# A down projection with seven block products in one period more, and the accumulators of both halves added up on GpSimd

## The chip, the cores and the metric

The kernel runs on one core of a Trainium2 chip. The metric is the device time of one execution in microseconds (us); three runs of the kernel before gave 1813.7, 1811.5 and 1813.31 us, median 1813.31. One further execution was profiled. In all that follows PE is TensorE (PEld its weight loads), DVE is VectorE, ACT is ScalarE, POOL is GpSimd, and SP is SyncE, which here only issues transfers.

## The reference

A block with a memory-augmented attention and, behind it, a feed-forward part; the change lies in the latter. With S = 2048 rows, D = 576 and F = 4608, all in float32:

```
h = _layernorm(x) * (1 + cb) + sb
g = silu(h @ w_gate)            # 2048 x 4608
u = h @ w_up
x = x + gb * ((g * u) @ w_down) # down projection, 2048 x 576
```

## The kernel before

The feed-forward part fills the time from about 640 us to the end. The 2048 rows are worked off in two halves of 1024, `t` = 0 and 1, and in each half the 4608 columns in 18 periods, `p` = 0 to 17 (`NPR` = 18), of 256 columns. A period has 14 steps, `k` = 0 to 13. In each step `step(z, m)` makes one of the seven products of a Strassen-Winograd scheme for gate (`z` = 0) or up (`z` = 1): seven matmuls of 128x512 into the PSUM banks A, B or C. `fin` makes from these the activations `sg`, and `prep_w` splits the weights for a step five steps ahead into a high part `wh` (ACT) and a low part `wl` (DVE, `wl <- O, wh`).

The down projection of a period is made one period later, between the steps. It too has two forms.

- `down`: seven block products. It has 14 chunks c, two for each of the products m in the order `POS` = 1, 4, 2, 5, 6, 7, 3. A chunk is six matmuls of 128x288 into a PSUM tile `pd` and one addition of `pd` to half of the accumulator `acc[m]`. In half 0 the odd chunks go another way: ACT loads the accumulator into PSUM beforehand (`preload`), the matmuls add to it, and ACT copies it back. The operands of the products are sums of blocks: `sum_a` (DVE) for the activations, `sum_d` (POOL, half 0 only) for the weights, which are then stored to DRAM for half 1.
- `plain`: the four blocks without the scheme. It has 8 chunks of twelve matmuls of 128x288, each followed by an addition on DVE into one of the four results `acc[2]`, `acc[3]`, `acc[4]` and `x11`.

Chunks alternate between two PSUM tiles, one buffer each (`dn0`, `dn1`), so chunk c+2 has to wait for the addition behind chunk c. Operands are split like the weights: `ah` and `dh` on ACT, `al <- sg, ah` and `dl <- dr, dh` on DVE. The tables CH, CH0, CHE and CHB say how many chunks follow each step.

Periods 0 to 15 use `down`, periods 16 and 17 use `plain`. Since `plain` adds to the four results, the seven accumulators have to be added up into these before: eight additions of 128x1152, `comb(t, j)` for j = 0 to 7, all on DVE, at steps 1 to 8 of period 17. They are acc2 += acc1, x11 += acc5, acc6 += acc1, acc5 += acc6, acc3 += acc5, acc7 += acc6, acc4 += acc7, x11 += acc7. The `plain` chunks of period 17 of half 0 are made in period 0 of half 1 ("across the border"); those of half 1 end the kernel, each followed by a store.

Everything is emitted in the order of this loop (the schedule is manual), so each engine works off its instructions in just that order. POOL has no instruction after period 17 of half 0.

Of the kernel before, what the change touches and what calls it, by code (L numbers as in the profile page):

```python
# [11 lines left out]
ALU = mybir.AluOpType  # L12
# [22 lines left out]
PF = 5  # L35
NSG = 7
CH = (1, 1, 1, 1, 2, 1, 0, 1, 1, 1, 1, 2, 1, 0)
CH0 = (0, 0, 0, 1, 1, 1, 1, 1, 1, 1, 1, 0, 0, 0)
CHE = (0, 0, 0, 0, 0, 1, 1, 1, 1, 1, 1, 1, 1, 0)
CHB = (0, 0, 1, 1, 1, 1, 1, 1, 1, 1, 0, 0, 0, 0)  # L40
# [32 lines left out]
RB = 9  # L73
RL = (-10, -1, 0, 4, 4, 9, 10, 10, 12, 10, 11, 12, 15, 16)
SUMS = ((4, 3, 2, ALU.add), (5, 4, 0, ALU.subtract), (3, 0, 3, ALU.subtract), (6, 1, 5, ALU.subtract))
S1B, S2B, XB, WB = 3, 3, 2, 1


# [5 lines left out]
def block(ctx: ExitStack, tc: tile.TileContext, x, wqk, wv, wo, beta, wgu, wgr, wd, c, crow, w_mod, w_mod0, w_mod1, w_modc, xt, out):  # L84
    nc = tc.nc
# [713 lines left out]
    op = pool(p2r, "op", side="right")  # L799
# [239 lines left out]
    NPR = NF // 2  # L1039
# [7 lines left out]
    def at(g, f):  # L1047
        sched.setdefault(g, []).append(f)
# [110 lines left out]
    def stage_r():  # L1159
        big = flat(yh12.rearrange("p a b c -> p (a b) c"))  # L1160
        ts = [big[:, 896 * i:896 * i + 896].rearrange("p (a b) -> p a b", b=P) for i in range(3)]
        for b in range(RB):
            o, h, g, w = ts[b % 2], ts[2].bitcast(F32R), 22 * b, b % (NF // 4)
            at(max(0, g + RL[0]), lambda w=w, o=o: nc.sync.dma_start(o[:, 0:4], wgr[w]))
            for j, (d, x_, y_, op) in enumerate(SUMS):
                at(max(0, g + RL[1 + j]), lambda o=o, d=d, x_=x_, y_=y_, op=op: nc.gpsimd.tensor_tensor(o[:, d], o[:, x_], o[:, y_], op=op))
# [135 lines left out]
    def sum_o(p, z, j, eng=nc.gpsimd):  # L1302
        o = O[p, z]
        d, a, b, op = SUMS[j]
        if eng is nc.vector:
# [15 lines left out]
    def load_d(t, p):  # L1321
# [4 lines left out]
        else:  # L1326
            nc.sync.dma_start(r[:, :NS[p]], wdD[p][:, :NS[p]])

# [99 lines left out]
        nc.vector.tensor_tensor(PA[d], PA[a], PA[b], op=op)  # L1428

    PA, acc, x11 = {}, {}, {}  # L1430
    NS = [7] * (NPR - 2) + [4] * 2

    def new_acc(accp, ms):
        for m in ms:
# [72 lines left out]
    def comb(t, j):  # L1507
        d, b = ((2, 1), (0, 5), (6, 1), (5, 6), (3, 5), (7, 6), (4, 7), (0, 7))[j]
        d = acc[d] if d else x11[t]
        nc.vector.tensor_tensor(d, d, acc[b], op=ALU.add)  # L1510

    def is_plain(t, p):
        return p >= NPR - 2

    with tc.manual_schedule():
        SB.append(S1B)
# [69 lines left out]
        for i in range(4):  # L1586
            for h in range(2):
                for c in range(WC):
# [5 lines left out]
                    if n in SS:  # L1594
                        j = SS.index(n)
# [33 lines left out]
        for t in range(2):  # L1629
            for p in range(NPR):  # L1630
                end = p == NPR - 1
                last = t == 1 and end
                dl = 2 if t == 0 and p == 0 else 0
                nx = (p + 1) % NPR
                tn = t if nx else t + 1
                if t == 0 and p == 1:
                    p7.close()
                    accq = pool(p4, "acq")
                    new_acc(accq, (1, 6, 7))
                    x2p = pool(p6, "x2p")  # L1640
                    g2 = prep2(x2p)
                if t == 0 and p == NPR - 1:
                    now[0] = PTK[0]
                    run(g2)
                    p6.close()
                if end:
                    load_x11(t)
                chunk = 0
                for k in range(14):
                    z, m = ZM[k]  # L1650
                    todo, later[:] = later[:], []
                    while nw < len(seq) and nw <= n + PF + (t == 0 and k == 7):
                        prep_w(*seq[nw])
                        nw += 1
                    n += 1
                    for f in todo:
                        f()
                    while outs:
                        outs.pop(0)()
                    if prev is not None and not is_plain(*prev):  # L1660
                        for c in range(chunk, chunk + CH[k] + CH[(k + 1) % 14]):
                            if not PRE:
                                preload(*prev, c)
                    while acts:
                        acts.pop(0)()
                    if dl and k in HP:
                        y_here(6 + HP.index(k))
                    if k != 1 or prev is not None:
                        step(z, m)
                    if k == 1 and prev is not None:  # L1670
                        PA[0, 1] = AC[0, 1]
                    if t == 0 and p == NPR - 1 and k in (7, 9, 10, 11, 12, 13) or t == 1 and p == 0 and k == 1:
                        load_y(1, ACT_OP[m])
                    swap = t == 1 and p == 0
                    if not last and k == (6 if swap else 7 - PF):
                        load_o(tn, nx, 0)
                        if dl:
                            for i in range(2):
                                nc.sync.dma_start(xD[3][:, 2 * i:2 * i + 2, :], x3[i])
                    elif not last and k == (14 - PF if tn else 8):  # L1680
                        load_o(tn, nx, 1)
                    if k == 2 + swap and (t or p):
                        load_r(p, 1)
                    elif not last and k == 9:
                        load_r(nx, 0)
                    if t == 0:
                        if k == 1 and p:
                            load_d(0, p)
                        elif not dl and k == 3:
                            mul_d(p, 0)  # L1690
                            mul_d(p, 1)
                        if not dl and k in (4, 5) and p < NPR - 2:
                            sum_d(p, 2 * k - 8)
                            sum_d(p, 2 * k - 7)
                        if tn == 0 and 5 <= k < 9:
                            sum_o(nx, 0, k - 5)
                        elif tn == 0 and k in (10, 11):
                            sum_o(nx, 1, 2 * k - 20)
                            sum_o(nx, 1, 2 * k - 19)
                        if k == 0 and p == 0:  # L1700
                            store_o(p, 0)
                            store_o(p, 1)
                        elif k == 11 and tn == 0:
                            store_o(nx, 0)
                        elif k == 13 and tn == 0:
                            store_o(nx, 1)
                        if k == (5 if end else 12 + dl // 2):
                            nc.scalar.dma_start(wdD[p][:, :NS[p]], RW[p][:, :NS[p]])
                    if t and k == 2 + 2 * swap:
                        load_d(1, p)  # L1710
                    if prev is not None and is_plain(*prev):
                        if k in (0, 2):
                            ij = (1, 0) if k == 0 else (0, 1)
                            prep_a(prev[1] % 2, ij, PA[ij])
                        if (CHE if t == 0 else CHB if p == 0 else CH0)[k]:
                            f = plain(*prev, chunk)
                            if f:
                                late[k + 3] = f
                            chunk += 1
                        due(k)  # L1720
                    elif prev is not None:
                        for j in range(4):
                            if k == KS[j]:
                                sum_a(j)
                        if k == 0:
                            prep_a(prev[1] % 2, 2, PA[1, 0])
                        for j, kk in KA:
                            if k == kk:
                                prep_a(prev[1] % 2, j, PA[ASRC[j]])
                        for _ in range(CH[k]):  # L1730
                            down(*prev, chunk)
                            chunk += 1
                    if end and 1 <= k < 9:
                        comb(t, k - 1)
                    if p == 0 and (t, k) in RS:
                        load_res(t, RS[t, k])
                    if is_plain(t, p):
                        if k in DK[t == 0 and end]:
                            j = DK[t == 0 and end].index(k)
                            prep_d(p, (j // 2, j % 2), j)  # L1740
                    elif k >= 7:
                        prep_d(p, POS[k - 7], WSLOT[POS[k - 7]])
                    for ij, kk, j in (((0, 0), 11, 1), ((1, 1), 13, 4)):
                        if k == kk:
                            prep_a(p % 2, ij if is_plain(t, p) else j, AC[ij])
                    now[0] = k
                    if t == 0 and k in G2 and p > 1:
                        next(g2, None)
                for k in sorted(late):
                    due(k)  # L1750
                PA.clear()
                PA.update(AC)
                prev = (t, p)
# [86 lines left out]
```

## Time and profile before

| | us |
|---|---|
| median of three runs | 1813.31 |
| profiled execution, its time | 1815.41 |
| its span | 1813.4 |
| PE busy in the span | 1786.3 (99%) |
| DVE busy | 1485.3 (82%) |
| ACT busy | 1086.7 (60%) |
| POOL busy | 672.6 (37%) |
| end of half 0's period 17, start of half 1 | 1189.2 |
| `comb` on DVE, half 0 | 1159.2 to 1179.2 |
| `comb` on DVE, half 1 | up to 1786.0 |

The span is what the profiler saw from the first to the last instruction; the execution's own time is 2.0 us longer. Times in the profile's rows count from the start of the span. A PE that is busy 99% of the time says that some matmul was under way all the time; what a change on PE is worth is read from the distance between the starts of matmuls.

### The profile page before, as it was taken

To read this page: it belongs to the slowest core of one execution; us is meant where nothing else is said; L and a number is where in the kernel's file an instruction comes from. 1 tells how busy PE (TensorE), PEld (TensorE's weight loads), DVE (VectorE), ACT (ScalarE), POOL (GpSimd) and SP (SyncE) were. 2 spreads that over 40 slices of the span, in tenths; PEclk is the share of its full clock that TensorE was granted. 3 is DMA by queue.
4 is the path that set the end of the run, shared out by engine and by line. 5 is a ranking of instruction groups with operands and counts; after the bars stand their busy time and mean duration, and the time that the engine had idled before them with its cause. 6 is when DMAs were issued, how large, how long until landed. Compare 5 with 4: busy or idle time off the path is not lost.

```text
span 1813.4 us, 31453 instructions
## 1 busy us (share of the span) xinstructions
PE 1786.3 (99%) x10627; PEld 1519.1 (84%) x10627; DVE 1485.3 (82%) x3365; ACT 1086.7 (60%) x2374; POOL 672.6 (37%) x1111
## 2 busy tenths in 40 slices
PE   7999999999999999999999999999999999999999
PEld 5888866777777888888888888888888888888888
DVE  7556388888886899889889889858888888888886
ACT  4334398878775567777777777534544544544542
POOL 3444077775467656656656655300000000000000
PEclk9999999999999999999999999999999999999999
DMA  7768766667557655455455354494333333324331
GB/s 273 266 225 289 262 206 194 195 197 231 164 169 238 207 179 176 141 178 177 139 181 174 116 175 145 159 308 153 104 107 124 94 98 130 104 83 130 107 103 53
DMA packets 146115, 306.26 MB, mean 169 GB/s; under 512 B 30916, under 2 KB 61764, under 8 KB 144164
## 3 DMA queue, kind: packets, MB, share of 16 engines
q1 hardware_dynamic: 134772, 260.19, 46.0%
q10 hardware_dynamic: 11184, 44.07, 6.0%
q8 instruction: 85, 1.39, 0.3%
q14 instruction: 74, 0.61, 0.1%
HBM read 198.69 MB, written 104.94 MB: 167 GB/s over the span
## 4 chain that ended last, share of the span: by engine, by line
PE 93%; DMA 2%; DVE 1%; ACT 1%; issue 1%; SPq 1%; POOL 0%; ACTq 0%; DVEq 0%; POOLq 0%
PE A L1357 25%; PE pd L1476 20%; PE C L1357 13%; PE B L1357 6%; PE pp L113 6%; PE s L219 4%; PE av L746 3%; PE pv L113 3%; PE s L722 3%; PE pw L866 3%; PE pd L1496 3%; PE pn L934 1%; ACT Pt L729 1%; PE pm L551 1%; DVE junk L224 1%; PE px L767 1%
## 5 line engine op out<-in xcount | busy, mean ns | idle before, releaser
L1357 PE MATMUL A<-y,wh 128*128 128x512 f32 x1152 | 404.5, 392 | 0.7 <-ACT cu L1386 0.7
L1484 DVE TENSOR_TENSOR acc<-acc,pd 128x576 f32<-128x576 f32 x327 | 245.2, 750 | 74.8 <-PE pd L1476 67.2
L1476 PE MATMUL pd<-dh,ah 128*128 128x288 f32 x896 | 264.7, 295 | 0.0
L1476 PE MATMUL pd<-dh,al 128*128 128x288 f32 x896 | 263.3, 294 | 0.0
L1476 PE MATMUL pd<-dl,ah 128*128 128x288 f32 x896 | 263.2, 294 | 0.0
L224 DVE CUSTOM_DVE_ANT_0 junk<-s,tri 128x512 bf16<-128x512 f32 (+1 forms) x480 | 207.3, 484 | 55.9 <-PE s L219 41.7
L1357 PEld LDWEIGHTS A<-y,wh 128*128 128x128 f32 x1152 | 216.3, 188 | 40.1 <-ACT cu L1386 1.1
L1318 DVE TENSOR_TENSOR wl<-O,wh 128x256 fp32r<-128x256 f32 x504 | 240.8, 481 | 2.1 <-ACT wh L1317 1.4
L1357 PE MATMUL A<-y,wl 128*128 128x512 f32 x576 | 225.7, 392 | 0.0
L729 ACT ACTIVATE Pt<-s 128x512 f32<-128x512 f32 (+1 forms) x352 | 182.6, 558 | 44.4 <-PE s L722 28.7
L1357 PE MATMUL C<-y,wh 128*128 128x512 f32 x576 | 202.5, 392 | 0.0
L1317 ACT CAST wh<-O 128x256 fp32r<-128x256 f32 x504 | 198.1, 405 | 0.3 <-DVE y L1188 0.3
L1476 PEld LDWEIGHTS pd<-dh,ah 128*128 128x128 f32 x896 | 168.2, 188 | 18.6 <-ACT pd L1452 4.0
L1422 DVE TENSOR_TENSOR al<-sg,ah 128x512 fp32r<-128x512 f32 x240 | 177.3, 739 | 6.7 <-ACT ah L1421 6.4
L1311 POOL TENSOR_TENSOR O<-O 128x128 f32<-128x128 f32 x280 | 154.4, 585 | 75.3 <-DMA O<-in_wgu_dram 36.9
L1476 PEld LDWEIGHTS pd<-dl,ah 128*128 128x128 f32 x896 | 168.2, 188 | 14.9
L1476 PEld LDWEIGHTS pd<-dh,al 128*128 128x128 f32 x896 | 168.0, 188 | 0.0
L1421 ACT CAST ah<-sg 128x512 fp32r<-128x512 f32 x240 | 149.0, 621 | 26.1 <-DVE sg L1381 25.3
L1357 PEld LDWEIGHTS C<-y,wh 128*128 128x128 f32 x576 | 108.0, 188 | 19.1
L1357 PEld LDWEIGHTS A<-y,wl 128*128 128x128 f32 x576 | 108.2, 188 | 15.0
L1357 PE MATMUL C<-y,wl 128*128 128x512 f32 x288 | 112.8, 392 | 0.0
L1357 PE MATMUL A<-y,wr 128*128 128x512 f32 x288 | 112.1, 389 | 0.0
(398 smaller groups left out, 4144.1 us busy)
## 6 DMA issues: line engine op xcount, KB each, us to landing
wr<-rD SPq DMA_DIRECT2D x216, 112.0 KB
O<-in_wgu_dram SPq DMA_DIRECT2D x36, 512.0 KB
oD<-O ACTq DMA_DIRECT2D x36, 512.0 KB
O<-oD SPq DMA_DIRECT2D x36, 512.0 KB
O<-in_wgu_dram SPq DMA_DIRECT2D x36, 384.0 KB
y<-yD SPq DMA_DIRECT2D x11, 1024.0 KB
ks<-kD SPq DMA_DIRECT2D x72, 144.0 KB
kD<-fh SPq DMA_DIRECT2D x16, 512.0 KB
```

Of the source, the lines that this page charges most:

```text
L113: nc.tensor.matmul(ps, lhsT=a, rhs=b, start=(k == 0), stop=(k == 13))
L219: nc.tensor.matmul(bank[:, n * (h - h0):n * (h - h0) + n], lhsT=qst[b][0:108, h, 128 * i:128 * i + 128], rhs=kst[b][0:108, h // 2, 0:n], s ...
L224: nc.vector.tensor_tensor_reduce(junk[:, :n], bank[:, n * (h - h0):n * (h - h0) + n], tri[:, L - n:], 1.0, -3e38, op0=ALU.add, op1=ALU.max ...
L729: nc.scalar.activation(pt[:, h:h + per, :n], bank[:, :n * per].rearrange("p (a b) -> p a b", a=per), AF.Exp, scale=SCALE)
L1311: eng.tensor_tensor(o[:, d, i, s_], o[:, a, i, s_], o[:, b, i, s_], op=op)
L1317: nc.scalar.copy(wh, o)
L1318: later.append(lambda: nc.vector.tensor_tensor(wl, o, f32(wh), op=ALU.subtract))
L1357: nc.tensor.matmul(bank, lhsT=a, rhs=b, start=(first and n == 0), stop=(n == 6), skip_group_check=not first)
L1421: nc.scalar.copy(ah, src)
L1422: later.append(lambda: nc.vector.tensor_tensor(al, src, f32(ah), op=ALU.subtract))
L1476: nc.tensor.matmul(pd[:, i, :288], lhsT=a[:, tk], rhs=w, start=(add and k == 0), stop=(k == 2), skip_group_check=not add)
L1484: nc.vector.tensor_tensor(o, o, pd[:, :, :288], op=ALU.add)
```

## The change

Period 16 uses `down` in both halves; only period 17 is `plain`. With it come: the eight `sum_d` instructions of POOL for period 16 (half 0), four `sum_a`, and seven instead of four pairs of operands for activations and weights; the weight block of period 16 that is stored and loaded again holds seven slots instead of four. The eight additions `comb` go from DVE to POOL. In half 0 they are emitted at steps 10, 12 and 13 of period 17 and steps 0 to 4 of the next half's period 0, in half 1 at steps 6, 9, 10, 11, 13, 12, 13, 13 of period 17 (table CB). In half 0's period 17 the chunks follow a table of their own, CHD, which starts at step 3.

```diff
+CHD = (0, 0, 0, 1, 1, 1, 2, 1, 2, 1, 2, 1, 2, 0)
+CB = ((10, 12, 13, 14, 15, 16, 17, 18), (6, 9, 10, 11, 13, 12, 13, 13))
...
-    NS = [7] * (NPR - 2) + [4] * 2
+    NS = [7] * (NPR - 1) + [4]
...
     def comb(t, j):
         d, b = ((2, 1), (0, 5), (6, 1), (5, 6), (3, 5), (7, 6), (4, 7), (0, 7))[j]
         d = acc[d] if d else x11[t]
-        nc.vector.tensor_tensor(d, d, acc[b], op=ALU.add)
+        nc.gpsimd.tensor_tensor(d, d, acc[b], op=ALU.add)
 
     def is_plain(t, p):
-        return p >= NPR - 2
+        return p == NPR - 1
...
+                ch = CHD if end and t == 0 else CH
...
-                        for c in range(chunk, chunk + CH[k] + CH[(k + 1) % 14]):
+                        for c in range(chunk, chunk + ch[k] + ch[(k + 1) % 14]):
...
-                        if not dl and k in (4, 5) and p < NPR - 2:
+                        if not dl and k in (4, 5) and not end:
...
-                        for _ in range(CH[k]):
+                        for _ in range(ch[k]):
                             down(*prev, chunk)
                             chunk += 1
-                    if end and 1 <= k < 9:
-                        comb(t, k - 1)
+                    if end or p == 0 and t:
+                        for j, c in enumerate(CB[t if end else 0]):
+                            if c == (k if end else k + 14):
+                                comb(t if end else 0, j)
```

How this moves instructions shows in the order in which the engines get them. In the rows below acc_8836, 8837, 8838 and 8839 are acc2 to acc5, acc_9097, 9098 and 9099 are acc1, acc6 and acc7, xw is x11, dr is the weight block.

POOL before, its last rows, from half 0's period 16 to the end of the program:

```order
L1332 TENSOR_TENSOR dr__15722<-dr__15722,gbB 128x144 x8
L1311 TENSOR_TENSOR O<-O 128x128 x16
L1332 TENSOR_TENSOR dr__16111<-dr__16111,gbB 128x144 x8
L1836 UNCONDITIONAL_BRANCH
L1836 ISA
```

POOL now, the same stretch up to the last addition of half 0:

```order
L1334 TENSOR_TENSOR dr__15722<-dr__15722,gbB 128x144 x8
L1341 TENSOR_TENSOR dr__15722<-dr__15722 128x144 x8
L1313 TENSOR_TENSOR O<-O 128x128 x16
L1334 TENSOR_TENSOR dr__16131<-dr__16131,gbB 128x144 x8
L1510 TENSOR_TENSOR acc_8836<-acc_8836,acc_9097 128x1152
L1510 TENSOR_TENSOR xw<-xw,acc_8839 128x1152
L1510 TENSOR_TENSOR acc_9098<-acc_9098,acc_9097 128x1152
L1510 TENSOR_TENSOR acc_8839<-acc_8839,acc_9098 128x1152
L1510 TENSOR_TENSOR acc_8837<-acc_8837,acc_8839 128x1152
L1510 TENSOR_TENSOR acc_9099<-acc_9099,acc_9098 128x1152
L1510 TENSOR_TENSOR acc_8838<-acc_8838,acc_9099 128x1152
L1510 TENSOR_TENSOR xw<-xw,acc_9099 128x1152
```

The eight additions stand behind one another on POOL with nothing between them, and eight more follow for half 1, where the queue was empty.

DVE before, from the last plain chunk of half 0's period 16 to the first addition behind a plain chunk of period 17 (steps 12 and 13 of period 17 and 0 to 2 of half 1):

```order
L1500 TENSOR_TENSOR xw<-xw,pd 128x576
L1318 TENSOR_TENSOR wl<-O,wh 128x256
L1377 TENSOR_TENSOR sg<-A,sg 128x512
L1318 TENSOR_TENSOR wl<-O,wh 128x256
L1346 TENSOR_TENSOR dl<-dr__16111,dh 128x288
L1422 TENSOR_TENSOR al<-sg,ah 128x512
L1318 TENSOR_TENSOR wl<-O,wh 128x256
L1422 TENSOR_TENSOR al<-sg,ah 128x512
L1380 TENSOR_TENSOR cu<-C,tb 128x512
L1381 TENSOR_TENSOR sg<-cu,sg 128x512
L1318 TENSOR_TENSOR wl<-O,wh 128x256
L1500 TENSOR_TENSOR acc_8836<-acc_8836,pd 128x576
```

DVE now, the same place, from the addition behind chunk 12 of period 16:

```order
L1486 TENSOR_TENSOR acc_8837<-acc_8837,pd 128x576
L1320 TENSOR_TENSOR wl<-O,wh 128x256
L1379 TENSOR_TENSOR sg<-A,sg 128x512
L1320 TENSOR_TENSOR wl<-O,wh 128x256
L1348 TENSOR_TENSOR dl<-dr__16131,dh 128x288
L1424 TENSOR_TENSOR al<-sg,ah 128x512
L1320 TENSOR_TENSOR wl<-O,wh 128x256
L1424 TENSOR_TENSOR al<-sg,ah 128x512
L1382 TENSOR_TENSOR cu<-C,tb 128x512
L1383 TENSOR_TENSOR sg<-cu,sg 128x512
L1320 TENSOR_TENSOR wl<-O,wh 128x256
L1502 TENSOR_TENSOR acc_8836<-acc_8836,pd 128x576
```

The row of the first chunk of period 17 has the same ten in front of it; what is new is the first row, which completes half of acc3 and with it is waited for by the fifth of POOL's additions. The second al is the operand that the first plain chunk needs.

DVE before, the end of the program, from the last `comb`:

```order
L1510 TENSOR_TENSOR xw<-xw,acc_9099 128x1152
L1318 TENSOR_TENSOR wl<-O,wh 128x256
L1500 TENSOR_TENSOR xw<-xw,pd 128x576
L1377 TENSOR_TENSOR sg<-B,sg 128x512
L1500 TENSOR_TENSOR xw<-xw,pd 128x576
L1346 TENSOR_TENSOR dl<-dr__22844,dh 128x288
L1422 TENSOR_TENSOR al<-sg,ah 128x512
L1380 TENSOR_TENSOR cu<-C,tc 128x512
L1381 TENSOR_TENSOR sg<-cu,sg 128x512
L1377 TENSOR_TENSOR sg<-A,sg 128x512
L1422 TENSOR_TENSOR al<-sg,ah 128x512 x2
L1380 TENSOR_TENSOR cu<-C,tb 128x512
```

DVE now, the same end (a few rows further):

```order
L1348 TENSOR_TENSOR dl<-dr__22914,dh 128x288
L1486 TENSOR_TENSOR acc_9099<-acc_9099,pd 128x576
L1486 TENSOR_TENSOR acc_8837<-acc_8837,pd 128x576
L1424 TENSOR_TENSOR al<-sg,ah 128x512
L1382 TENSOR_TENSOR cu<-C,tc 128x512
L1383 TENSOR_TENSOR sg<-cu,sg 128x512
L1486 TENSOR_TENSOR acc_8837<-acc_8837,pd 128x576
L1379 TENSOR_TENSOR sg<-A,sg 128x512
L1424 TENSOR_TENSOR al<-sg,ah 128x512 x2
L1382 TENSOR_TENSOR cu<-C,tb 128x512
L1383 TENSOR_TENSOR sg<-cu,sg 128x512
L1502 TENSOR_TENSOR acc_8836<-acc_8836,pd 128x576
```

The additions behind chunks 11 to 13 (acc7, twice acc3) now lie in the last two steps, and five of POOL's additions wait for them or for one another from there on.

## The prediction

> **What bounds the kernel now.** I read the page first, then busy time by stretches, one period each, around the border between the halves, then the instructions in order of time at the border and at the end.
>
> ```profile
> PE 1786.3 (99%) x10627; PEld 1519.1 (84%) x10627; DVE 1485.3 (82%) x3365; ACT 1086.7 (60%) x2374; POOL 672.6 (37%) x1111
> PE 93%; DMA 2%; DVE 1%; ACT 1%; issue 1%; SPq 1%; POOL 0%; ACTq 0%; DVEq 0%; POOLq 0%
> ```
>
> The first line is busy time, the second the chain that ended last: PE carries 93% of it. In the next rows (us, then PE, PEld, DVE, ACT, POOL) stand period 16 of half 0, in which seven products are made for period 15, then period 17 and period 0 of half 1, in which plain chunks are made.
>
> ```profile
> 1120.72:1154.19 33.47, 33.47 (x184) 29.41 (x182) 28.07 (x49) 24.62 (x52) 13.42 (x24) 1.00 0.47 149
> 1154.19:1189.23 35.04, 35.04 (x196) 31.02 (x194) 30.80 (x45) 13.73 (x33) 7.19 (x8) 1.00 0.67 232
> 1189.23:1224.27 35.04, 35.04 (x196) 31.01 (x194) 20.07 (x39) 13.81 (x33) 0.00 (x0) 1.00 0.88 295
> ...
> 1192.40 0.39 PE L1357 MATMUL A<-y,wh 128*128 128x512 f32 x1
> ...
> 1193.99 0.29 PE L1496 MATMUL pd<-dh,ah 128*128 128x288 f32 x1
> ...
> 1195.57 0.39 PE L1357 MATMUL B<-y,wh 128*128 128x512 f32 x1
> ```
>
> PE fills each period at full clock (1.00). The matmul rows show its pace: a step of seven takes 1193.99 - 1192.40 = 1.59 us, a plain chunk of twelve 1195.57 - 1193.99 = 1.58, one of its matmuls 0.13, a chunk of six 0.79. Fourteen steps and eight plain chunks are 34.9, fourteen steps and fourteen chunks of six 33.3; the periods measure 35.04 and 33.47. So PE has no gap at the border, and the other engines count only where they make it wait. At the end DVE is just in time:
>
> ```profile
> PEld pd L1496 <- DVE al L1422: 0.2, 1, 0.2
> ```
>
> This is the only wait of PE in the last 44 us.
>
> **The parts of the change.**
>
> *Seven products for period 16.* Per half a period of 35.04 becomes one of 33.47: 1.57 us less, -3.14 in all (24 matmuls at 0.13 say the same). The work that comes with it (sum_a, three more al, dl, ah and dh, ACT's copies and sum_d in half 0, the larger weight block's transfers) lies in every earlier period already and leaves PE full there, as the 33.47 row shows; I cost it at nothing. If the cover went, CHD's denser chunks would show it first, where ACT has one step and one chunk to empty and refill a PSUM tile.
>
> *The additions leave DVE.*
>
> ```profile
> L1510 DVE TENSOR_TENSOR acc<-acc,acc x12: 1344/1351/1653, 1159.2 to 1781.4; 128x1152 f32<-128x1152 f32 x12
> ```
>
> Eight times 1.35 us per half, 10.8, but PE did not wait for them: gain nothing.
>
> *What one costs on POOL.* No POOL instruction of 128x1152 is in the trace. The nearest:
>
> ```profile
> L1166 POOL TENSOR_TENSOR yh<-yh 128x128 f32<-128x128 f32 x36 | 16.2, 460 | 13.7 <-DMA yh<-in_wgr_dram 12.7
> L784 POOL TENSOR_TENSOR o<-o,tmp 128x288 f32<-128x288 f32 x24 | 19.3, 804 | 16.7 <-DVE tmp L783 16.7
> L956 POOL TENSOR_TENSOR o<-nm,r 128x576 f32<-128x576 f32 x12 | 14.0, 1168 | 0.9
> L1027 POOL TENSOR_TENSOR woraw<-woraw,gaB 128x576 f32<-128x576 f32 x5 | 7.1, 1419 | 0.0
> ```
>
> From 288 to 576 columns the last row gives (1.419 - 0.804)/288 = 2.135 ns a column, which fits the first row too (0.804 - 160 x 0.002135 = 0.462). For 1152: 1.419 + 576 x 0.002135 = 2.65 us. The row of 1.168 gives (1.168 - 0.804)/288 = 1.26 ns and 1.9 us; it takes r by the row, while ours reads two whole tiles, as L1027 does. I take 2.65 and keep 1.9 as the low end.
>
> *What it does to DVE.* Here lies the price.
>
> ```profile
> 268.43 0.25 DVE L775 RECIPROCAL r<-px 128x16 f32<-128x16 f32 x1
> 268.72 1.17 DVE L776 TENSOR_TENSOR r<-r,omg 128x16 f32<-128x16 f32 x1
> 268.42 1.42 POOL L1027 TENSOR_TENSOR woraw<-woraw,gaB 128x576 f32<-128x576 f32 x1
> ...
> L776 DVE TENSOR_TENSOR r<-r,omg x32: 174/190/1170, 240.9 to 569.8; 128x16 f32<-128x16 f32 x32
> ...
> 167.87 1.56 DVE L435 CUSTOM_DVE_ANT_0 wmc<-wmc,srow 128x576 f32<-128x576 f32 x1 [3.85 <-DMA wmc<-in_w_modc_dram]
> 167.52 1.28 POOL L530 TENSOR_TENSOR x<-x,rw 64x512 f32<-64x512 f32 x1
> 168.88 1.68 POOL L531 TENSOR_TENSOR x<-x,rw 64x512 f32<-64x512 f32 x1
> ...
> 1064.24 0.98 DVE L1428 TENSOR_TENSOR sg<-sg 128x512 f32<-128x512 f32 x1
> 1065.14 0.74 DVE L1484 TENSOR_TENSOR acc<-acc,pd 128x576 f32<-128x576 f32 x1
> ...
> 1063.73 5.21 POOL L1339 TENSOR_TENSOR dr__14836<-dr__14836 128x144 f32<-128x144 f32 x8
> ```
>
> L776, both inputs in SBUF, takes 0.19 as a rule. Beside POOL's instruction from 268.42 to 269.84 it took 1.17 and ended at 269.89: it stood until POOL was through. DVE instructions with an input from PSUM (268.43, or 0.74 at 1065.14) pass unharmed. At 168.88 POOL stood instead: DVE ended at 169.43, POOL 1.13 later, where its like takes 1.28. Beside short POOL instructions DVE loses little: 0.98 for the usual 0.69 at 1064.24, since one column costs 2.1 ns and 144 of them 0.31. A POOL addition of 2.65 thus holds the next DVE instruction with two SBUF inputs, and all behind it, for up to 2.65. Alternating, one such pair costs 2.65 - 0.15 on POOL and DVE's own time less 0.14 (1.17 = 1.12 left + 0.19 - 0.14).
>
> The Trainium skill, "SBUF — State Buffer", sections "SBUF: two separate sides" and "Who interferes with whom", says the same as a rule: the port pair that VectorE shares with GpSimd is an exclusive lock, held for a whole instruction, and a VectorE instruction with two SBUF inputs needs it. By that rule the change is slower; the trace agrees to 0.05 us. Its page "GPSIMD Engine Reference", section "Elementwise — side-by-side cycle accounting", gives 2.6 cycles at 1.2 GHz, 2.17 ns a column, against 2.135 here; by it the addition would be an estimated 2.7 us.
>
> DVE's rows at the border and the end, for their times:
>
> ```profile
> 1190.37 0.45 DVE L1346 TENSOR_TENSOR dl<-dr__16111,dh 128x288 fp32r<-128x288 f32 x1
> 1191.34 0.42 DVE L1318 TENSOR_TENSOR wl<-O,wh 128x256 fp32r<-128x256 f32 x1
> 1192.15 0.69 DVE L1422 TENSOR_TENSOR al<-sg,ah 128x512 fp32r<-128x512 f32 x1 [0.39 <-ACT ah L1421]
> 1192.76 0.69 DVE L1380 TENSOR_TENSOR cu<-C,tb 128x512 f32<-128x512 f32 x1
> 1193.48 0.69 DVE L1381 TENSOR_TENSOR sg<-cu,sg 128x512 f32<-128x512 f32 x1
> ...
> L1479 ACT COPY acc<-pd x105: 635/642/647, 649.4 to 1152.8; 128x576 f32<-128x576 f32 x105
> ```
>
> wl, dl, al and sg<-cu read SBUF twice; cu, sg<-A and the additions of pd read PSUM.
>
> *The border.* Zero is the end of chunk 13 in half 0's period 17. PE then makes four steps, 6.36, and plain chunk 0, whose sixth matmul needs the second al: 6.36 + 5 x 0.13 = 7.0. The third addition (j = 2) needs chunk 9, which ended four chunks and two steps earlier, at -6.3; ACT's copy makes it -5.4. It runs to -2.8, j = 3 behind one wl (0.28) to 0.0. DVE then has wl, al, cu, sg<-cu and the addition of chunk 12 (0.28 + 0.61 + 0.61 + 0.72 + 0.75), so acc3 is whole at 3.0 and j = 4 starts. From there POOL has four additions back to back; between them DVE gets one wl, dl, al, wl, and then the al: 2.65 + 0.28 + 2.5 + 0.31 + 2.5 + 0.55 + 2.5 + 0.28 + 0.6 = 12.2. It is ready at 15.2, PE waits 8.2.
>
> *The end.* Zero is the end of chunk 13 in half 1's period 17. Chunk 7 ended at -12.7, so j = 1 runs from -11.3 to -8.6. DVE's al behind it ends at -8.0; dl, sg<-C, an addition, wl, al and the addition of chunk 9 take 3.3 more, so j = 2 starts at -4.7 and ends at -2.05; with a dl between, j = 3 ends at 0.8, with an al, j = 5 at 3.8. The sg<-cu held by it ends at 4.35, the addition of chunk 13 at 5.0: j = 4 to 7.65. Then al, j = 6 to 10.7, al, j = 7 to 13.75, sg<-cu to 14.3, and the addition of plain chunk 0 to 15.0. Chunk 2 needs its PSUM tile; unhindered it would start at two steps and two chunks, 6.3. PE loses 8.7. The last additions and stores follow as before.
>
> **The sum.** -3.14 + 8.2 + 8.7 = +13.8: the profiled execution's 1815.41 becomes 1829.2. It stood 2.1 above the median, so the median goes from 1813.31 to 1827.1.
>
> **The rivals.**
>
> *POOL's additions hide; not slower.* One mechanism: at border and end DVE is let through beside them, for instance because POOL lets go of the port between pieces of a long tile. Then -3.14 remains: 1810.2. For it: DVE is busy only 20.07 of 35.04 us in half 1's period 0, and POOL's 8 x 2.65 = 21 us fit beside 35. Against: 1.17 for L776. It decides below some 1.5 us of hold per addition: with 1.9 the six in a chain at the border cost 4.5 less than with 2.65, leaving 3.7 there, and the seven at the end 5.3 less, leaving 3.4. That is 4.0 above no change, and thirteen additions give this back when each is another 0.3 shorter.
>
> *The additions take 1.9 us* (row L956): -3.14 + 3.7 + 3.4 = +4.0, 1817.
>
> *DVE loses more than one turn in each pair.*
>
> ```profile
> 554.65 0.74 POOL L1149 TENSOR_TENSOR yh<-yh 96x256 f32<-96x256 f32 x1
> 555.34 0.63 POOL L733 TENSOR_SCALAR_AFFINE_SELECT Pt<-Pt 128x512 f32<-128x512 f32 x1
> 554.79 1.46 DVE L1054 TENSOR_TENSOR yq<-yo,yq 32x256 fp32r<-32x256 f32 x1
> ```
>
> Here DVE waited for two POOL instructions, not one. At the border all five of its instructions would follow j = 7: 3.0 + 10.6 + 2.3 = 15.9, a wait of 8.9. If the additions themselves stretch to 3.0, seven at the end cost 2.5 more, six at the border 2.1: about +18.5, 1832.
>
> **How the numbers follow.** No change can be told from one under 0.2%, 3.6 us. Chances: the hold at 2.65, 0.60, 1822 to 1830; shorter additions, 0.17, 1815 to 1822; lost turns, 0.13, above 1830; hidden, 0.10, around 1810. Hidden counts as same (0.06) or faster (0.04), as its 3.14 is just under the bound; of the short ones 0.04 are same. That gives faster 0.04, same 0.10, slower 0.86. The range 1814 to 1833 leaves out the hidden case and some of the lost turns.
>
> **What the profile of the changed kernel would show.** The two periods with seven products at 33.5 us apart from waits: the gain. L1510 on POOL at 2.65: the price. wl, dl and al of 2.5 to 3.1 us at the border and the end, beside cu and sg<-A at 0.69: the hold. A gap on PE of about 8 us inside plain chunk 0 at the border, and one as long in the last 30 us: the sum. I am wrong if DVE's rows stay at 0.42 and 0.69 beside L1510, or if al comes early enough because POOL started its last four additions later than the al.

## The result, and the profile after

The changed kernel takes 1830.82 us (median of five executions, 1826.63 to 1832.31) against 1813.31 before (five, 1811.5 to 1816.15). The ratio is 1.0094, with a 95% interval of 1.0081 to 1.0107: slower by some 17 us. The profiled execution took 1830.78 us, its span is 1829.0.

The lines of the page on busy time and on the chain that ended last, and the same stretches as before: period 17 of half 0, which now makes seven products, and the following stretch with the border.

```profile
PE 1787.2 (98%) x10603; PEld 1517.5 (83%) x10603; DVE 1507.9 (82%) x3374; ACT 1101.0 (60%) x2400; POOL 726.9 (40%) x1135
PE 92%; DVE 3%; ACT 2%; DMA 2%; issue 1%; SPq 0%; POOL 0%; ACTq 0%; DVEq 0%; POOLq 0%
...
1153.77:1187.33 33.56, 33.56 (x183) 29.25 (x182) 28.98 (x42) 23.41 (x49) 16.84 (x12) 1.00 0.67 231
1187.33:1232.00 44.67, 36.28 (x193) 31.91 (x192) 30.47 (x42) 14.35 (x34) 11.16 (x4) 0.92 0.74 239
```

Although sixteen additions of 1.35 us left DVE and only the operands of one more period of seven products came to it, it is busy 23 us longer than before; this is waiting inside its instructions, as the next rows show (with the same work and no such waiting, in e1 below, DVE is busy for 1480.9 us). Period 17 measures 33.56 where it was 35.04: the gain is there. In the next stretch PE is idle for 8.4 us, and its granted clock is 0.92 where it was 1.00. The groups of the additions, and the rows at the border (POOL, DVE, PE):

```profile
L1512 POOL TENSOR_TENSOR acc<-acc,acc 128x1152 f32<-128x1152 f32 x12 | 33.2, 2781 | 598.3 <-DVE acc L1486 582.9 <-ACT acc L1481 10.5 <-DVE wl L1320 3.3
L1512 POOL TENSOR_TENSOR xw<-xw,acc 128x1152 f32<-128x1152 f32 x4 | 12.8, 3206 | 4.2 <-DVE acc L1486 4.0 <-ACT acc L1481 0.2
...
1189.39 8.22 POOL L1512 TENSOR_TENSOR acc<-acc,acc 128x1152 f32<-128x1152 f32 x3 [3.33 <-DVE wl L1320]
1197.57 3.06 POOL L1512 TENSOR_TENSOR xw<-xw,acc 128x1152 f32<-128x1152 f32 x1
...
1189.78 2.56 DVE L1320 TENSOR_TENSOR wl<-O,wh 128x256 fp32r<-128x256 f32 x1
1192.26 2.88 DVE L1348 TENSOR_TENSOR dl<-dr__16131,dh 128x288 fp32r<-128x288 f32 x1
1195.07 3.09 DVE L1424 TENSOR_TENSOR al<-sg,ah 128x512 fp32r<-128x512 f32 x1
1198.08 2.83 DVE L1320 TENSOR_TENSOR wl<-O,wh 128x256 fp32r<-128x256 f32 x1
1200.83 0.68 DVE L1424 TENSOR_TENSOR al<-sg,ah 128x512 fp32r<-128x512 f32 x1
...
1192.36 0.29 PE L1498 MATMUL pd<-dh,ah 128*128 128x288 f32 x1
...
1201.56 0.61 PE L1498 MATMUL pd<-dh,al 128*128 128x288 f32 x1 [8.39 <-DVE al L1424]
1201.97 0.44 PE L1498 MATMUL pd<-dh,ah 128*128 128x288 f32 x1
1202.21 0.44 PE L1498 MATMUL pd<-dl,ah 128*128 128x288 f32 x1
```

Four DVE instructions with both inputs in SBUF, between POOL's four additions, take 2.56 to 3.09 us instead of 0.42 to 0.69; the al behind the last is back at 0.68. PE stands in the sixth matmul of the first plain chunk, 8.39 us. The last rows show something else: matmuls now start 0.24 us apart, where before it was 0.13. The stretches of 2 us behind show why (columns as in the prediction's first table, the granted clock is the third number from the right):

```profile
1196.00:1198.00 2.00, 0.00 (x0) 0.00 (x0) 2.00 (x1) 0.00 (x0) 2.00 (x2) 0.96 1.03 333
1198.00:1200.00 2.00, 0.00 (x0) 0.00 (x0) 2.00 (x2) 0.00 (x0) 2.00 (x1) 0.50 1.03 299
...
1202.00:1204.00 2.00, 2.00 (x9) 1.90 (x9) 1.42 (x4) 1.51 (x3) 0.00 (x0) 0.50 1.09 264
...
1206.00:1208.00 2.00, 2.00 (x15) 1.87 (x14) 0.61 (x1) 0.70 (x2) 0.00 (x0) 1.00 0.95 316
```

The clock falls to 0.50 while PE stands idle, and stays there for some 3 us after it goes on. By the starts of the matmuls the first plain chunk and the step B behind it take 13.25 us, 1192.36 to 1205.61, where the kernel before takes 3.20: 10.05 us more, 8.4 of waiting and 1.65 of slow clock. At the end the rows of POOL, DVE and PE are:

```profile
1804.08 5.63 POOL L1512 TENSOR_TENSOR acc<-acc,acc 128x1152 f32<-128x1152 f32 x2 [1.34 <-issue]
1809.68 3.10 POOL L1512 TENSOR_TENSOR xw<-xw,acc 128x1152 f32<-128x1152 f32 x1
...
1804.47 5.79 DVE L1424 TENSOR_TENSOR al<-sg,ah 128x512 fp32r<-128x512 f32 x2
1810.19 0.68 DVE L1382 TENSOR_TENSOR cu<-C,tb 128x512 f32<-128x512 f32 x1
1810.90 2.42 DVE L1383 TENSOR_TENSOR sg<-cu,sg 128x512 f32<-128x512 f32 x1
...
1803.26 0.29 PE L1498 MATMUL pd<-dh,ah 128*128 128x288 f32 x1
...
1805.31 0.40 PE L1498 MATMUL pd<-dh,ah 128*128 128x288 f32 x1 [1.50 <-ACT ah L1423]
...
1810.32 0.61 PE L1498 MATMUL pd<-dh,al 128*128 128x288 f32 x1 [4.48 <-DVE al L1424]
...
1815.05 0.44 PE L1498 MATMUL pd<-dh,ah 128*128 128x288 f32 x1
```

Two al take 5.79 us beside POOL. During POOL's last addition cu, which has an input in PSUM, takes its usual 0.68 us, and sg<-cu behind it, with two inputs in SBUF, 2.42. PE waits 1.5 and 4.5 us inside plain chunk 0, and runs at half pace from 1810.3 to 1815.6. Chunk 2 starts at 1815.05, behind the 24 matmuls of chunks 0 and 1. At full pace that is 3.2 us after the start of chunk 0 at 1803.26; here it is 11.8, so 8.6 us are lost by then, and 0.3 more until the clock is back.

### The profile page after: what moved, and what is told of

It reads as the page before. It is cut to its first block, busy times and chain, and to the rows that moved or that the text cites. A ratio compares the mean times of both kernels' runs of the same rounds, so it can differ in the third digit from the quotient of the medians.

```text
span 1829.0 us, 31495 instructions
## 1 busy us (share of the span) xinstructions
PE 1787.2 (98%) x10603; PEld 1517.5 (83%) x10603; DVE 1507.9 (82%) x3374; ACT 1101.0 (60%) x2400; POOL 726.9 (40%) x1135
## 4 chain that ended last, share of the span: by engine, by line
PE 92%; DVE 3%; ACT 2%; DMA 2%; issue 1%; SPq 0%; POOL 0%; ACTq 0%; DVEq 0%; POOLq 0%
PE A L1359 25%; PE pd L1478 20%; PE C L1359 12%; PE B L1359 6%; PE pp L115 5%; PE s L221 4%; PE av L748 4%; PE pv L115 3%; PE s L724 3%; PE pw L868 3%; PE pd L1498 2%; ACT Pt L731 1%; PE pn L936 1%; PE pm L553 1%; PE px L769 1%
## 5 line engine op out<-in xcount | busy, mean ns | idle before, releaser
L1486 DVE TENSOR_TENSOR acc<-acc,pd 128x576 f32<-128x576 f32 x348 | 260.7, 749 | 79.5 <-PE pd L1478 71.5
L1478 PE MATMUL pd<-dh,ah 128*128 128x288 f32 x952 | 281.4, 296 | 0.0
L1478 PE MATMUL pd<-dh,al 128*128 128x288 f32 x952 | 279.8, 294 | 0.0
L1478 PE MATMUL pd<-dl,ah 128*128 128x288 f32 x952 | 279.7, 294 | 0.0
L1512 POOL TENSOR_TENSOR acc<-acc,acc 128x1152 f32<-128x1152 f32 x12 | 33.2, 2781 | 598.3 <-DVE acc L1486 582.9
L1320 DVE TENSOR_TENSOR wl<-O,wh 128x256 fp32r<-128x256 f32 x504 | 251.6, 503 | 1.4 <-ACT wh L1319 0.9
L1478 PEld LDWEIGHTS pd<-dh,ah 128*128 128x128 f32 x952 | 178.7, 188 | 20.1 <-ACT pd L1454 4.7
L1424 DVE TENSOR_TENSOR al<-sg,ah 128x512 fp32r<-128x512 f32 x246 | 190.0, 773 | 3.9 <-ACT ah L1423 3.7
L1478 PEld LDWEIGHTS pd<-dl,ah 128*128 128x128 f32 x952 | 178.7, 188 | 15.7
L1478 PEld LDWEIGHTS pd<-dh,al 128*128 128x128 f32 x952 | 178.5, 188 | 0.0
```

The lines of the kernel that those rows point to most:

```text
L1320: later.append(lambda: nc.vector.tensor_tensor(wl, o, f32(wh), op=ALU.subtract))
L1424: later.append(lambda: nc.vector.tensor_tensor(al, src, f32(ah), op=ALU.subtract))
L1478: nc.tensor.matmul(pd[:, i, :288], lhsT=a[:, tk], rhs=w, start=(add and k == 0), stop=(k == 2), skip_group_check=not add)
L1486: nc.vector.tensor_tensor(o, o, pd[:, :, :288], op=ALU.add)
```

## The experiments

The theory (hold): a POOL instruction that reads SBUF holds a DVE instruction with two SBUF inputs until it ends, so operands of matmuls come late. Rivals: the gaps come without a hold, from the length or the late place of POOL's chain and what waits for its results, or from the new order of the seven products. Where the expectations use letters, H is the hold and the others are such rivals. A median over executions takes in what the first 1190 us happen to do: the first plain chunk of half 1 starts between 1189 and 1194 us in profiled executions of kernels that are alike up to there. So each run is also compared by the stretch from that matmul to the end of its span, in its one profiled execution; before it is 1813.4 - 1193.99 = 619.4 us, after 1829.0 - 1192.36 = 636.6. With the gain of one period (1.5 us in half 1) and nothing lost it would be 617.9.

| kernel | median us | ratio to before, interval | border to end, us |
|---|---|---|---|
| before | 1813.31 | | 619.4 |
| after | 1830.82 | 1.0094 (1.0081 to 1.0107) | 636.6 |
| e1, POOL only writes | 1810.55 | 0.9985 (0.9977 to 0.9994) | 619.6 |
| e2, quarters | 1811.9 | 0.9995 (0.9987 to 1.0003) | 620.3 |
| e3, additions on DVE | 1818.48 | 1.0027 (1.0016 to 1.0037) | 626.5 |
| e4, only to POOL | 1822.29 | 1.0052 (1.0039 to 1.0065) | 621.1 |
| f1, halves | 1819.51 | 1.0035 (1.0021 to 1.0048) | 627.3 |
| f2, border whole | 1823.36 | 1.0055 (1.0043 to 1.0067) | 630.3 |
| f3, eighths and DVE | 1811.99 | 0.9987 (0.9979 to 0.9996) | 620.3 |
| f4, no idle PE | 1826.56 | 1.0073 (1.0061 to 1.0085) | 634.6 |

Each ratio is to executions of the kernel before on the same chip: their median was 1813.48 beside e1 to e4 and 1813.43 beside f1 to f4.

**e1: POOL keeps as long a chain, but reads nothing.** Each addition becomes three fills of the same accumulator; the sums are left out.

```diff
-        nc.gpsimd.tensor_tensor(d, d, acc[b], op=ALU.add)
+        for _ in range(3):
+            nc.gpsimd.memset(d, 0.0)
```

> Each of POOL's sixteen additions is replaced by three POOL memsets of the same accumulator (the sums are left out), at the same place in the queue and behind the same waits; three of 128x1152 should occupy POOL about 3 us, a little longer than the 2.65 to 3.2 of an addition. Theory H (a POOL instruction that reads SBUF holds the next DVE instruction with two SBUF inputs to its end): nothing is read, so wl, dl and al stay at 0.42, 0.45 and 0.69, PE has no gap, and the gain of 3.1 us shows: 1810 us. Rival L (the eight sums form a chain that simply ends too late for the plain chunks, whatever the port does): the chain is as long as before or longer, so PE's gaps of 8 us stay: 1829 to 1832. Rival S (seven products for period 16 and the table CHD themselves cost PE time): also stays, about 1829.

Rows of POOL and of DVE at the border, then all that PE waited for from 1140 to 1240 us:

```profile
1177.42 16.27 POOL L1513 MEMSET acc<- 128x1152 f32 x15 [1.16 <-ACT acc L1481]
...
1187.42 0.69 DVE L1424 TENSOR_TENSOR al<-sg,ah 128x512 fp32r<-128x512 f32 x1 [0.41 <-ACT ah L1423]
...
PE A L1359 <- DMA wr<-rD: 1.2, 2, 0.9
```

POOL takes 16.27 us for five sets of fills, 3.3 each, longer than the changed kernel's 2.7 to 3.2 per addition, through the whole border, and DVE keeps its 0.69. One fill is short, 1.06 us; that alone does not spare DVE, for in e2 below pieces of 0.98 us that do read stretch al from 0.69 to 1.30. Chain length is refuted as the cause, reading is needed for the hold. The order of all other work is the changed kernel's, so neither that order nor the seven products make the gaps. The median is 2.9 us under before: about the gain of the two periods, once nothing is held. The profiled execution does not show both gains: from the border to the end it takes 619.6 us and not 617.9, as PE now waits twice, 1.2 us in all, for the transfer of wr, which was not expected. The Trainium skill, "SBUF — State Buffer", section "Who interferes with whom", says that a VectorE instruction with two SBUF inputs contends with a GpSimd instruction that reads SBUF and not with one that only writes it; after and e1 show both sides of that sentence, 3.09 us against 0.69 for al.

**e2: the same additions in quarters.** The same reading and adding, in four instructions of 288 columns.

```diff
-        nc.gpsimd.tensor_tensor(d, d, acc[b], op=ALU.add)
+        for q in range(4):
+            e = 288
+            u, v = (x.rearrange("p a b -> p (a b)")[:, e * q:e * q + e] for x in (d, acc[b]))
+            nc.gpsimd.tensor_tensor(u, u, v, op=ALU.add)
```

> Each addition on POOL is cut into four of 128x288, nothing else changes. POOL needs 4 x 0.80 = 3.2 us for a sum instead of 2.65, but one piece holds DVE for at most about 0.65. Theory H: PE's gaps shrink from 8.4 and 6.0 us to under 1 each, and the time falls to 1811 to 1814 us. Rival L: the chain gets longer by 4 x 0.55 us per half, so the gaps grow: 1832 or more.

The group of the pieces, DVE at the border, and PE's only wait there and at the end:

```profile
L1515 POOL TENSOR_TENSOR acc<-acc,acc 128x288 f32<-128x288 f32 x48 | 45.5, 982 | 578.9 <-DVE acc L1486 577.8 <-ACT acc L1481 0.9
...
1189.73 0.95 DVE L1320 TENSOR_TENSOR wl<-O,wh 128x256 fp32r<-128x256 f32 x1
...
1193.76 1.30 DVE L1424 TENSOR_TENSOR al<-sg,ah 128x512 fp32r<-128x512 f32 x1
...
PE pd L1498 <- DVE al L1424: 0.6, 1, 0.6
...
PE pd L1498 <- DVE al L1424: 0.7, 1, 0.7
```

An addition now takes POOL 4 x 0.982 = 3.9 us, a good microsecond longer, and still PE's waits fall from 8.4 and 6.0 to 0.6 and 0.7 us. DVE gets a turn after about 1 us instead of 2.8. What costs is how long one POOL instruction is.

**e3: the additions on DVE, at the changed kernel's places.**

```diff
-        nc.gpsimd.tensor_tensor(d, d, acc[b], op=ALU.add)
+        nc.vector.tensor_tensor(d, d, acc[b], op=ALU.add)
```

> The sixteen additions go back to DVE, at the places in the program where the changed kernel has them on POOL. Theory H: no row of wl, dl or al above 0.8 us at the border; there the gap of PE shrinks from 8.4 to under 1.5 us. At the end five additions of 1.35 stand in DVE's queue ahead of the first al of the plain chunks, so a gap of about 5 us stays. In all about 1815 to 1819 us, 12 to 15 faster than the changed kernel. Rival S: at least 1825, as the seven products are still there.

PE's waits in the last 67 us:

```profile
PE pd L1498 <- DVE al L1424: 3.8, 1, 3.8
PE pd L1498 <- ACT ah L1423: 1.3, 1, 1.3
```

The time is in the range expected. The border is nearly free (0.8 us more by the matmuls' starts); at the end the additions lie ahead of the last al and, with the slow clock behind the gap, cost 7.8 us against before, close to the 8.7 that they cost on POOL (both from the first matmul of the last plain chunks to the last one, 12.7 us before). At the end the place is bad whoever adds: the additions can start only when the last chunks have ended, and the operands of chunk 0 are due just then.

**e4: the kernel before, with its additions on POOL.** Periods 16 and 17 stay plain, the eight additions stay at steps 1 to 8 of period 17.

```diff
-        nc.vector.tensor_tensor(d, d, acc[b], op=ALU.add)
+        nc.gpsimd.tensor_tensor(d, d, acc[b], op=ALU.add)
```

> The kernel before with its eight additions per half moved from DVE to POOL and nothing else: two plain periods, additions at steps 1 to 8 of period 17. Theory H: in half 0 the additions run back to back after the multiplications of the weight block, DVE gets one instruction with two SBUF inputs per addition, and PE gets a gap of 8 to 10 us inside period 17 (the plain chunks wait for their additions on DVE). In half 1 POOL can start earlier, DVE has room, gap under 1 us. In all +9 to +12 us: 1822 to 1826. Rival L: the sums end well before period 17's own plain chunks, which come a period later, but those of period 16 stand in between; rival S: no seven products in period 16, so no loss: 1813.

Rows of POOL and DVE in half 0's period 17, PE's longest waits there, and its only wait in the last 77 us:

```profile
1159.35 14.35 POOL L1510 TENSOR_TENSOR acc<-acc,acc 128x1152 f32<-128x1152 f32 x5
...
1159.59 3.16 DVE L1422 TENSOR_TENSOR al<-sg,ah 128x512 fp32r<-128x512 f32 x1
1162.68 5.71 DVE L1318 TENSOR_TENSOR wl<-O,wh 128x256 fp32r<-128x256 f32 x2
...
PE pd L1496 <- DVE acc L1500: 3.0, 2, 1.6
...
PE pd L1496 <- DVE al L1422: 1.0, 1, 1.0
```

The hold appears without the seven products, and the kernel is 8.8 us slower by the medians. Its place was not as expected: in half 0 four small waits (3.5 us together) and not one large, in half 1 one of 1.0. The profiled execution's span is only 3.3 us above before's profiled one, so this trace accounts for part of the median's loss; the rest is open.

**f1: halves.** As e2, with two pieces of 576 columns.

> Each GpSimd addition is cut into two instructions of 576 columns; nothing else changes. By the hold theory a piece holds VectorE for at most 1.42 us instead of 2.69, and VectorE gets a turn between any two pieces: the gap at the border shrinks from 8.4 us to about 3.2, those at the end from 6.0 to 1.5 to 2.6, and the time lies near 1816 to 1818 us, between the quarters (1811.9) and the whole additions (1830.8). By the rival that the end of GpSimd's chain decides, nothing shrinks and the time stays at 1829 to 1832. On the clock: if only gaps of more than about 4 us of an idle TensorE lower it, it stays at 1.00 here; if shorter gaps do too, the windows behind the border's gap show about 0.5.

PE's wait at the border, those at the end (two of three), and the clock behind each:

```profile
PE pd L1498 <- DVE al L1424: 3.5, 1, 3.5
...
PE pd L1498 <- DVE al L1424: 1.2, 1, 1.2
PE pd L1498 <- ACT ah L1423: 0.6, 1, 0.6
...
1200.00:1202.00 2.00, 2.00 (x6) 1.54 (x5) 2.00 (x2) 0.91 (x2) 2.00 (x2) 0.50 1.07 296
...
1804.00:1806.00 2.00, 2.00 (x10) 2.00 (x10) 1.96 (x3) 0.62 (x1) 2.00 (x2) 0.50 0.00 0
```

The gaps lie between those of whole additions (8.4 and 6.0) and quarters (0.6 and 0.7), near the 3.2 and 1.5 to 2.6 expected. The time is 1.5 us over the range expected. From the border to the end it takes 7.0 us more than e2; the waits make up 4.2 of this, and the other 2.8 are about what the clock cost, which fell twice, for 3.41 us each time: here a gap of 3.5 us sufficed, and so did two of 0.6 and 1.2 close together.

**f2: half 0 whole, half 1 in quarters.** (The loop of e2 with n = 4 for t = 1 and 1 for t = 0.)

> Half 0's eight additions stay whole on GpSimd, half 1's are cut into quarters: the border's loss alone is left. If the two losses are independent, the border's share is what its rows said, 8.4 us of waiting and some 1.4 us of lowered clock behind it, on top of the version with quarters everywhere (1811.9): 1821 to 1822 us, and the end shows less than 1 us of gaps. If the loss at the end were a consequence of the border (a delay carried through half 1), the time would be near 1812 + 17 = 1829; if the lowered clock costs nothing beside the gap, 1820.

PE's waits at the border and at the end, and the stretch of slow clock at the border:

```profile
PE pd L1498 <- DVE al L1424: 8.4, 1, 8.4
...
PE pd L1498 <- DVE al L1424: 0.7, 1, 0.7
...
1192.78:1203.02 10.24, 4.84 (x15) 4.17 (x16) 8.66 (x9) 1.51 (x3) 4.46 (x2) 0.50 1.03 308
```

From the border to the end it takes 630.3 us, e2 takes 620.3: the border's share is 10.0. By the matmuls' starts the border loses 10.8 here, of which 2.5 are slow clock, and 0.8 in e2. The slow clock costs more than the changed kernel's 1.65 behind a gap of the same 8.4 us: 4.84 us of it lie behind the gap and not 3.1. The rest of the changed kernel's 636.6, 6.3, goes with its end. The median, 1823.36, is 1.4 over what was expected. The losses are independent: nothing of the border's delay shows at the end, where only 0.7 us of waiting is left.

**f3: a version against both losses.** Half 0's additions in eighths on POOL; of half 1's, five in eighths on POOL and the last three on DVE in halves, just ahead of the plain chunks that need them.

```diff
+        if t and i is None and j in (4, 6, 7):
+            return
...
+        if i is not None:
+            o = d[:, 2 * i:2 * i + 2]
+            nc.vector.tensor_tensor(o, o, acc[b][:, 2 * i:2 * i + 2], op=ALU.add)
+            return
...
             if c == 0:
                 flush()
+            if c < 6:
+                comb(1, (4, 4, 6, 6, 7, 7)[c], c % 2)
```

> Half 0's additions on GpSimd in eighths (144 columns), half 1's additions 0, 1, 2, 3 and 5 on GpSimd in eighths, and its additions 4, 6 and 7 on VectorE in halves behind the last chunks 0 to 5, just ahead of the chunks that need them. By the hold theory no gap of over 0.5 us is left and the 3 us of the seven products are kept: 1810 to 1811.5 us, at or a little under the version with quarters. If short GpSimd instructions have a cost of their own (64 pieces instead of 8), gaps come back and it is slower than the 1811.9 of the quarters, 1813 or more.

PE's waits at the border and at the end, and the stretch behind the border:

```profile
PE A L1359 <- DMA wr<-rD: 1.4, 2, 0.7
...
PE pd L1498 <- DVE al L1424: 0.4, 1, 0.4
...
1190.00:1225.00 35.00, 33.58 (x189) 29.33 (x187) 21.92 (x40) 13.46 (x32) 14.23 (x27) 1.00 0.94 296
```

The gaps of the hold are gone, but the time, 1811.99, is 0.5 over the range expected and cannot be told from e2's. What is late next is a transfer: the matmuls of A wait for wr, twice, as in e1. In this stretch the transfers are at a share of 0.94, before at 0.88. It may be that loads which were just in time now come late for a PE that is ahead; that is not shown, as e3 has the same 0.94 there and no such wait. From the border to the end e1, e2 and f3 are no faster than before (619.6 to 620.3 against 619.4): the gain of half 1 is taken back by these waits and by the short ones for al. Both e1 and f3 are faster than before, by 0.13 to 0.15%; f3 is the one with all its sums, by an amount that its interval just separates from nothing.

**f4: the changed kernel with a busy PE in the gaps.** Extra matmuls, whose result the first real one overwrites.

```diff
+        if p == NPR - 1 and not (b or h or c):
+            for _ in range(30 if t else 55):
+                nc.tensor.matmul(pd[:, 0, :288], lhsT=AP[p % 2, (0, 0)][0][:, :128],
+                                 rhs=DP[p % 2, (0, 0)][0], start=True, stop=True)
```

> The changed kernel, with extra products issued ahead of the first last-period chunk of each half, into the same accumulator, which the first real product then starts anew: 55 of 0.13 us (7.2 us) in the border's gap of 8.4 us, 30 (3.9 us) in the end's gap of 4.5. They fill gaps in which TensorE otherwise stands idle, and VectorE and GpSimd do as before. If the idle time is what lowers the granted clock from 1.00 to 0.50, the windows behind the gaps now show 0.9 or more and the time falls by the 1.2 to 1.4 us per gap, to about 1828 us, although work was added. If the clock falls for another reason, it falls again and the time is 1831 or, where the extra products end late, more.

PE's waits at the border and at the end, and the clock behind the border and at the end:

```profile
PE pd L1501 <- DVE al L1424: 1.4, 1, 1.4
...
PE pd L1501 <- DVE al L1424: 2.4, 1, 2.4
...
1198.00:1200.00 2.00, 0.65 (x5) 0.41 (x4) 2.00 (x3) 0.00 (x0) 0.77 (x1) 1.00 1.00 325
...
1807.00:1809.00 2.00, 1.87 (x8) 1.87 (x9) 1.97 (x3) 0.00 (x0) 2.00 (x1) 0.50 0.00 0
```

With 7.2 us of added matmuls at the border the clock stays at 1.00 and the kernel is faster: 1826.56 against 1830.82. From the border (here the first extra matmul) to the end it is 2.0 us less. That the idle time lowers the clock is shown at the border, and not by one execution alone: the mean granted clock is 0.998 or 0.999 in all five of f4, and 0.994 or 0.995 in all five of the changed kernel. At the end the added work was too short: 2.4 us of idling were left, and the clock fell again. By the matmuls' starts the border's loss went down by 1.2 us; the 4.3 of the medians are more than these rows explain.

## Why the prediction was right

**The gain**, 3.14 us: the period measures 33.56 instead of 35.04, 1.48 less; in half 1, the stretch from the second plain chunk at the border to the first at the end measures 597.65 instead of 599.17, 1.52 less. All work that was costed at nothing stayed hidden here, CHD's chunks too: from 640 us on PE has no wait but those at the border and the end. In e1 and f3, where nothing is held, 1.2 and 1.4 us of waiting for wr come up; whether the larger transfers cause them is open.

**One addition on POOL**, 2.65 us from the line through two shorter rows: the first one, with DVE little in its way, takes 2.69, the twelve of one group 2.78, and the four into x11 3.21. The low end of 1.9 fell, as did the rival built on it.

**The hold** is shown by e1 (no reading, no hold), e2 and f1 (the waits follow the length of one instruction, not of the chain). DVE got its turn between any two additions, as assumed; the rival in which it loses more than that did not show.

**The border**: j = 4 started 3.4 us after the end of chunk 13 (said 3.0), the al was ready at 15.5 (15.2), PE waited 8.4 (8.2). The step that fell short is the one that took a wait as the whole loss: PE went on at half its clock, 1.65 us more.

**The end**: 8.7 us were forecast, some 8.9 came, but not in the way forecast. The addition of chunk 0 was done 13.9 us after the end of chunk 13 (said 15.0), so chunk 2's tile would have held PE until then, a loss of 7.6. PE came later than that: it stood 6.0 us for ah and al inside chunk 0, resumed at 10.2, and at full pace would have been at chunk 2 at 12.7 and waited for the tile; at half pace it got there at 15.0. The dates of POOL and DVE were some 1 us too late, and the slow clock that no term had makes up for it: that the end's number came out is partly luck.

**The sum**: +13.8 was forecast, the profiled executions differ by 1830.78 - 1815.41 = 15.4. The 1.6 between are about the border's slow clock, which no term had. The other 2.1 us up to the measured median are the step from the profiled execution to the median: before's was 2.1 above its median, after's is at its own, so nothing should have been taken off. So the time, 1830.82, lies in the band that was given to lost turns, above 1830, though the mechanism was that of the hold.

The Trainium skill, "TensorE: Matmul & The Clock Gate", section "What's actually happening", states that a TensorE idle for a window of about 3.4 us drops to half rate and needs about as long a busy one to come back. By that rule alone the border's term would have been an estimated 1.7 us larger, half of 3.4. The trace agrees in the rate (0.50) and in the 3.1 us after the border's gap. It does not agree in the idle time needed: gaps of 2.4 us in f4, and of 0.6 and 1.2 in f1, were enough.

## What to carry to other kernels

Before moving an elementwise operation from VectorE to GpSimd, look at what VectorE does beside it: one long GpSimd instruction that reads SBUF adds up to its whole length to each VectorE instruction with two SBUF inputs, and to all that waits for those. If it has to move, cut it: here quarters made GpSimd's chain longer and took away nearly the whole loss (1830.8 to 1811.9 us). Each single wait of TensorE of 2.4 us or more cost more here than it shows, since matmuls behind it ran at half pace for a while.

## What the hardware showed that was not expected

- The granted clock falls to 0.50 during or shortly behind a gap of TensorE, and matmuls of 128x288 then start 0.24 us apart instead of 0.13 until it is back, 3.1 to 5.5 us after the gap. It fell at waits of 8.4, of 1.5 and 4.5 close together, of 1.3 and 3.8 close together (e3), of 3.5 and of 2.4 us, and behind 0.6 and 1.2 close together; not behind single ones of 1.4 (f4) and 0.7 (e2), nor behind two of 1.4 and 1.6 with 3.5 us of matmuls between them (e4). Filling a gap with useless matmuls made the kernel faster. The stretches at 0.50 last 3.41 us (f1 twice, f4), 6.82 or 6.83 (the changed kernel twice, e3) or 10.24 (f2), one, two or three times the same length, and they begin between 2 us after PE has stopped and 1.5 us after it has gone on, so the same gap of 8.4 us cost 1.65 us of slow clock in one execution and 2.5 in another. What exactly decides was not found out.
- A fill by GpSimd of 128x1152 takes 1.1 us (3.3 for three) and, in e1, holds up no VectorE instruction at the border or the end.
